# Expert weights loaded in halves, and slots narrowed to 3,264 columns

## The chip, the cores and the metric

The kernel runs on one core of one Trainium2 chip. All data is fp32. The metric is the device time of one execution in microseconds (us). A core has five engines with instruction queues of their own: PE (TensorE, matrix products), DVE (VectorE), ACT (ScalarE), POOL (GpSimd) and SP (SyncE, which here only issues DMAs). They meet through semaphores. DMAs that SP, ACT and POOL issue are carried out by the same 16 DMA engines. An indirect DMA (a scatter by row numbers) is issued by POOL.

## The reference

Two blocks in a row. The first is a linear recurrence over 768 steps for 4 batches and 8 heads of 48; the second routes each of the 3,072 resulting rows of 384 to one of 16 experts, chosen in two stages (group, then expert in the group), each expert being two matrices with a ReLU between.

```python
# recurrence: r, k, v are [4, 8, 768, 48], w and u are [8, 48]
for t in range(S):
    cur = einsum('bhd,bhe->bhde', u * kt, vt)
    y[:, :, t] = einsum('bhd,bhde->bhe', rt, state + cur)
    state = w * state + einsum('bhd,bhe->bhde', kt, vt)
x = y.transpose(0, 2, 1, 3).reshape(3072, 384)
# routing and experts: w1[g, e] is [384, 1024], w2[g, e] is [1024, 384]
for g in range(4):
    for e in range(4):            # the rows whose best group is g and best expert in it is e
        h = maximum(xg[mask_e] @ w1[g, e], 0)
        out[tok_idx] = (g_w * e_w)[:, None] * (h @ w2[g, e])
```

## The kernel before

**Recurrence.** The 768 steps are cut into 6 chunks of 128, which with 4 batches makes 24 tiles. A software pipeline runs 27 steps, `s` = 0 to 26 (loop at L852). In step `s` the kernel turns tile `s` (`turn`, L716), forms the scores of tile `s-1` (`scores`: matmul L730, masked copy L735), the values of tile `s-2` (`values`: matmuls L751, L758 and L770, copy `yT` L764 on ACT) and turns tile `s-3` back into rows (`back`, matmuls L795 and L803). Later steps also carry the routing of finished rows: logits, choice, gate, place, and then `rows` (L457), a POOL scatter of 128 rows with their gate and number into the DRAM tensor `x_sorted`, which holds one region per expert. All five engines follow a written order in this part; nothing is reordered.

**Which experts first.** After four chunks the two experts that have the most rows so far are picked (`pick_first`). Their weights are loaded while the recurrence still runs: w1 of the first at the start of step 21 (`load_w1`, L484: four DMAs of 384 KB, one for each 32 partitions, each row of 4 KB), its rows (`load_rows`, L548 and L554) and w2 (`load_w2`, L489: one DMA of 1,536 KB) at the end of step 21, w1 of the second at the start of step 24. The row load waits until the scatters of those rows have landed. SP issues these in order, so what stands behind a waiting DMA on SP waits too.

**Two places for weights.** `places[0]` is a pair of tiles of its own (`w` in the profile); `places[1]` lies over the buffers of k and r (`kall` and `rall`), which the recurrence no longer needs by then. Expert number `e` in the sorted order uses place `e % 2`. A second copy of w2 with the columns regrouped (`w_parts`) is made by ACT, and for the first expert partly by POOL (`w2_part`, L480, four copies an expert).

**Experts.** There are 17 items: the first 128 rows of the first expert (item 0, run inside the last steps of the recurrence), the rest of its rows (item 1), then one item for each of the other 15 experts. Rows of an item are columns of its matmuls: `columns` (L561) turns the rows on DVE, `up` (L596) makes two 128-blocks of the hidden layer from w1 at a call (`f` = 0, 2, 4, 6), ACT applies the ReLU (L600), and `down` (L617) makes one of three 128-blocks of the output (`d`), which ACT copies (L620). `SLOTS` says how many columns the item of the n-th expert has. Were an expert to have more rows than its slot, the rows beyond it would be done by a slow part at the end. PE and DVE follow the written order here too; the order of ACT, POOL and SP comes from the scheduler. PE's order for item `i` is

```python
up(i, 0); up(i, 2); down(i - 1, 1); up(i, 4); up(i, 6); down(i - 1, 2); down(i, 0)
```

with item 1 and the last item differing a little: item 1 has no output of an earlier item between, so `down(1, 0)` follows `up(1, 6)` at once. After `up(i, 6)` SP loads the rows of item `i + 2`, and after `down(i, 0)` it loads w1 and w2 of the expert that follows in the same place (`load_expert`). The output goes out by `pieces_out`: one POOL scatter (L656) for each 32 columns of the item, 104 in all, and for the last item by `rows_out`: two POOL scatters (L669), one of 128 rows and one of the rest.

**DMA bookkeeping.** DMAs issued by SP take their completion semaphores in turn from eight; before one is issued, SP waits until the DMA that last used its semaphore has landed.

Of the kernel before, what the change touches and what calls it, by code (L numbers as in the profile page):

```python
# [9 lines left out]
I32 = mybir.dt.int32  # L10
# [6 lines left out]

SLOTS = [256, 240, 233, 222, 216, 212, 206, 202, 199, 196, 193, 190, 187, 184, 178, 173]  # L20
CAP = max(SLOTS)
FOUR = 4

# [11 lines left out]
def kernel(  # L35
# [13 lines left out]
    nc = tc.nc  # L49
# [43 lines left out]
    def cst(shape, name, dtype=FP32):  # L93
        return const.tile(shape, dtype, name=name)
# [387 lines left out]
    def load_w1(e, i):  # L482
        for q in range(P // BL):
            nc.sync.dma_start(  # L484
                out=places[i][0][BL * q : BL * (q + 1)], in_=w1f[bass.ds(e, 1), q].rearrange("a p k f -> (a p) k f")
            )

    def load_w2(e, i):
        nc.sync.dma_start(out=places[i][1], in_=w2f[bass.ds(e, 1)].rearrange("a p k f -> (a p) k f"))  # L489

    def load_expert(e, i):

        load_w1(e, i)
        load_w2(e, i)
        return places[i]

    def transposed(x, dst):
# [18 lines left out]
    def parts(i):  # L516
        return [min(P, width(i) - a) for a in range(0, width(i), P)]
# [7 lines left out]
    def is_last(i):  # L525
        return i == len(ITEMS) - 1

    def padded(n):
        return -(-n // BL) * BL

    def load_rows(i, expert, queue, other=None):

# [30 lines left out]
    def keys_in(i):  # L563
        key = xgs.pop(i)[1]
        w = padded(width(i))
        ids = item_tile(i, [P, room(i) // BL], "ids", U32, bufs=4)
        gates = item_tile(i, [P, room(i) // BL], "gates", bufs=4)
        if is_last(i):
            for j, n in enumerate(parts(i)):
                nc.vector.tensor_scalar(  # L570
                    out=ids[0:n, j : j + 1], in0=key[0:n, j, ROW_ID : ROW_ID + 1], scalar1=float(N), scalar2=None,
                    op0=OP.add,
                )
                nc.vector.tensor_copy(gates[0:n, j : j + 1], key[0:n, j, ROW_GATE : ROW_GATE + 1])
# [49 lines left out]
    def turn_out(i, d0, d1):  # L624

        if d0 == 0:
            out_rows[i] = [
                (bank([P, DM], "pb"), item_tile(i, [P, DM], "yt", bufs=4)) for j in range(len(parts(i)))
            ]
        gates = keys_of[i][1]  # L630
# [32 lines left out]
    def rows_out(i, d0=0):  # L663
        turn_out(i, d0, KO)
        ids = keys_of[i][0]
        for j, n in enumerate(parts(i)):
            yt = out_rows[i][j][1]

            ins = nc.gpsimd.indirect_dma_start(  # L669
                out=out, out_offset=bass.IndirectOffsetOnAxis(ap=ids[0:n, j : j + 1], axis=0), in_=yt[0:n],  # L670
                in_offset=None, bounds_check=N - 1, oob_is_err=False,
            )
            tc.declare_no_dep(ins.ins, group="rows out", reason="no token comes twice")
            tc.add_to_no_dep_group("rows out", ins.ins)
# [170 lines left out]
    def expert_of(number, engines):  # L845
        return nc.values_load(
            number, engines=engines, min_val=0, max_val=GE - 1,
            skip_runtime_bounds_check_because="four bits of a whole number",
        )

    LAST = 3
    for s in range(NT + LAST):  # L852
        pieces = todo.pop(s, [])
# [39 lines left out]
        if s == FOUR * B + 5:  # L893
            first = expert_of(first_i[0:1, 0:1], (SP,))
            second = expert_of(first_i[0:1, 1:2], (SP,))
            load_w1(first, 0)
        if s == NT:
            columns(0)
            load_w1(second, 1)
        run("first")  # L900
        if s < NT:
            turn(s)
# [28 lines left out]
            values(s - 2)  # L931
        run("last")
        if s == FOUR * B + 5:
            load_rows(0, first, nc.sync)
            load_w2(first, 0)
            weights[0] = places[0]
        n = s - 3
        if n >= NT - B:
            row_logits(n)
# [48 lines left out]

    warm(13, bank([P, P], "idle"))
    load_rows(2, second, nc.sync)  # L990
    load_w2(second, 1)
    weights[1] = places[1]
    written.close()
    alive.close()
# [2 lines left out]
    with ExitStack() as moe:  # L997
        pools[1] = moe.enter_context(tc.tile_pool(name="moe", bufs=2, reuse_waits="tile"))
        w2_parts.append(pools[1].tile([P, FO, KO, P], FP32, bufs=1, name="w2_parts_1"))
        with tc.manual_schedule(engines={mybir.EngineType.PE, mybir.EngineType.DVE}):  # L1000
            columns(1)
            keys_in(0)
            pieces_out(0)
            keys_in(1)


            for i in range(1, len(ITEMS)):
                left_over = [lambda d=d: down(i - 1, d) for d in (1, 2)] if i > 1 else []

                def go_on():  # L1010
                    if left_over:
                        left_over.pop(0)()
                        if not left_over:
                            pieces_out(i - 1)

                up(i, 0)
                if is_last(i):
                    go_on()
                up(i, 2)
                go_on()  # L1020
                up(i, 4)
                up(i, 6)
                e = ITEMS[i][0] + 2
# [12 lines left out]
            rows_out(i, 2)  # L1036

# [229 lines left out]
```

## Time and profile before

| | |
|---|---|
| median of 4 runs | 433.42 us (431.75 to 434.56) |
| the profiled execution, its own time | 434.66 us |
| its span, first to last instruction | 432.9 us |
| mean granted TensorE clock in it | 0.989 |
| busy: PE, PEld, DVE, ACT, POOL | 412.7, 385.9, 183.6, 216.3, 202.4 us |
| DMA: packets, bytes, mean rate | 124,476, 86.67 MB, 200 GB/s |

Times in the trace are counted from the start of the span. PE is the matrix product, PEld the loading of its stationary operand; an fp32 product appears as two MATMUL records. The recurrence with its routing fills the span up to about 164 us, items 1 to 16 the rest. A wait put down to "remote" is one for a semaphore whose sender the profile could not place, and "issue" is time in which an engine waited for nothing that the profile shows. DMA share is the mean busy share of the 16 DMA engines; it can read a little over 1.

### The profile page before, as it was taken

How to read it: one execution, taken by the hardware profiler on the slowest of the kernel's cores; microseconds unless marked ns; L12 is line 12 of the kernel's file. 1: busy time of each engine (PE TensorE's matmuls, PEld its weight loads, DVE VectorE, ACT ScalarE, POOL GpSimd, SP SyncE). 2: the span in 40 equal slices, each digit the busy share in tenths (PEclk: the TensorE clock that was granted, in tenths of full speed). 3: DMA queues.
4: the chain of work that ended last, by engine and by line, in shares of the span. 5: the costliest groups of instructions: out<-in, count | busy, mean ns of one | idle time of the engine just before them, and what ended most of it. 6: DMA issues, size and time to landing. Idle time of an engine off the chain costs nothing. (4 is left out here: it accounts for less than half of the span.)

```text
span 432.9 us, 9930 instructions
## 1 busy us (share of the span) xinstructions
PE 412.7 (95%) x3649; PEld 385.9 (89%) x3649; DVE 183.6 (42%) x620; ACT 216.3 (50%) x505; POOL 202.4 (47%) x214
## 2 busy tenths in 40 slices
PE   7799999999989897999999999999999999999993
PEld 6688888888867697999999999999999999999993
DVE  6666879787948555030303303213213213303211
ACT  2796766777657311526335163463363464365340
POOL 6875557677670633030426245254254255335453
PEclk9999999999998999899999999999999999999998
DMA  9999999991196829997979779899899899999001
GB/s 173 212 249 267 301 246 209 217 185 40 46 231 186 201 82 238 249 221 199 247 170 278 154 217 258 191 253 225 220 257 223 224 247 250 227 262 273 21 25 35
DMA packets 124476, 86.67 MB, mean 200 GB/s; under 512 B 96998, under 2 KB 113565, under 8 KB 124420
## 3 DMA queue, kind: packets, MB, share of 16 engines
q1 hardware_dynamic: 112732, 69.05, 70.7%
q0 software_dynamic: 4960, 9.48, 6.8%
q10 hardware_dynamic: 6728, 7.44, 5.0%
q8 instruction: 30, 0.49, 0.5%
q14 instruction: 26, 0.21, 0.2%
HBM read 70.15 MB, written 16.44 MB: 200 GB/s over the span
## 5 line engine op out<-in xcount | busy, mean ns | idle before, releaser
L656 POOL DMA_INDIRECT out_dram<-yp,ids x104 | 101.2, 974 | 164.2 <-DVE yo L611 128.6
L617 PE MATMUL po<-hT,w_parts 128*128 128x128 f32 (+15 forms) x816 | 139.7, 328 | 2.0 <-ACT hT L600 2.0
L617 PEld LDWEIGHTS po<-hT,w_parts 128*128 128x128 f32 x816 | 133.8, 190 | 3.2 <-ACT hT L600 2.2
L649 DVE STREAM_TRANSPOSE yr<-yo 128x224 f32<-128x224 f32 (+3 forms) x48 | 22.0, 464 | 185.9 <-ACT yo L620 180.7
L596 PE MATMUL ph<-xe,w 128*128 128x128 f32 (+7 forms) x432 | 72.1, 322 | 1.5 <-issue 0.8
L596 PEld LDWEIGHTS ph<-xe,w 128*128 128x128 f32 x432 | 68.7, 190 | 2.8 <-issue 1.4
L596 PE MATMUL ph<-xe,kall 128*128 128x240 f32 (+7 forms) x384 | 70.2, 340 | 0.0
L600 ACT ACTIVATE hT<-ph 128x256 f32<-128x256 f32 (+15 forms) x68 | 33.5, 496 | 71.0 <-PE ph L596 50.1
L596 PEld LDWEIGHTS ph<-xe,kall 128*128 128x128 f32 x384 | 66.6, 193 | 1.0
L620 ACT COPY yo<-po 128x128 f32<-128x128 f32 (+15 forms) x51 | 16.2, 321 | 90.3 <-PE po L617 61.3
L705 ACT ACTIVATE am<-ident,du 128x128 f32<-128x128 f32 x192 | 58.7, 391 | 2.0 <-DVE du L697 1.8
L735 DVE COPY_PREDICATED am<-later,pa 128x512 f32<-128x512 uint32 x48 | 32.7, 728 | 16.1 <-PE pa L730 8.9
L480 ACT COPY w_parts<-rall 128x768 f32<-128x768 f32 x32 | 38.0, 1235 | 0.0
L457 POOL DMA_INDIRECT x_sorted<-xt,place_i x24 | 23.8, 994 | 25.4 <-DVE rb L822 14.0
L480 ACT COPY w_parts<-w 128x768 f32<-128x768 f32 x29 | 34.4, 1233 | 0.0
L691 POOL TENSOR_TENSOR dg<-rall,kall 128x768 f32<-128x768 f32 (+1 forms) x13 | 22.1, 1702 | 21.6 <-DVE du L697 21.1
L730 PE MATMUL pa<-rT,kT 48*128 48x128 f32 x384 | 30.2, 286 | 1.5 <-issue 1.4
L730 PEld LDWEIGHTS pa<-rT,kT 48*128 48x128 f32 x384 | 24.3, 187 | 4.2 <-issue 2.5
L758 PE MATMUL py<-am,vt 128*64 128x128 f32 x384 | 26.4, 279 | 0.0
L684 POOL TENSOR_TENSOR kh<-kall,T 128x768 f32<-128x768 f32 (+1 forms) x12 | 21.7, 1806 | 9.9 <-PE pu L770 3.6
L720 ACT COPY kT<-pk 128x512 f32<-128x512 f32 x24 | 14.0, 584 | 22.0 <-PE pk L716 19.7
L758 PEld LDWEIGHTS py<-am,vt 128*64 128x64 f32 x384 | 20.5, 136 | 4.2 <-issue 3.5
(146 smaller groups left out, 408.5 us busy)
## 6 DMA issues: line engine op xcount, KB each, us to landing
w<-in_moe_w_dram SPq DMA_DIRECT2D x32, 384.0 KB
w<-in_moe_w_dram SPq DMA_DIRECT2D x8, 1536.0 KB
kall<-in_moe_w_dram SPq DMA_DIRECT2D x32, 384.0 KB
rall<-in_moe_w_dram SPq DMA_DIRECT2D x8, 1536.0 KB
x_sorted<-nothing ACTq DMA_DIRECT2D x4, 1544.0 KB
rall<-in_r_dram SPq DMA_DIRECT2D x12, 384.0 KB
vt<-in_v_dram SPq DMA_DIRECT2D x12, 384.0 KB
kall<-in_k_dram SPq DMA_DIRECT2D x10, 384.0 KB
```

The source lines that it names most:

```text
L457: ins = nc.gpsimd.indirect_dma_start(out=xs_dram, out_offset=bass.IndirectOffsetOnAxis(ap=place_i[:, i : i + 1], axis=0), in_=xt[:, i, :], ...
L480: copy(w2_parts[e % 2][:, a : a + 2], w2[:, a : a + 2, :].rearrange("p f (c k) -> p f k c", k=KO))
L596: nc.tensor.matmul(ph[:, q, :], lhsT=w1[:, ko, P * (f + q) : P * (f + q + 1)], rhs=xe[:, ko, 0:w], start=(ko == 0), stop=(ko == KO - 1), s ...
L600: nc.scalar.activation(hTs[i][:, f : f + 2, 0:w], ph, AF.Relu)
L617: nc.tensor.matmul(po, lhsT=w2[:, fo, d, :], rhs=hT[:, fo, 0:w], start=(fo == 0), stop=(fo == FO - 1))
L649: nc.vector.transpose(yr[:, 0:b, :, d], y[:, d, 0:w].rearrange("p (b t) -> p b t", t=BL))
L656: ins = nc.gpsimd.indirect_dma_start(out=out_pieces, out_offset=bass.IndirectOffsetOnAxis(ap=ids[:, j : j + 1], axis=0), in_=yp[:, j], in_ ...
L691: engine.tensor_mul(dg, rts[g % RING][:, a0:a1, :, 0:D], kts[g % RING][:, a0:a1])
L705: nc.scalar.mul(am[:, e, hc, :], ident, dus[n // 2][:, n % 2, h : h + 1])
L730: nc.tensor.matmul(pa[e][:, hc, :], lhsT=kT[rows, hc, :], rhs=rT[rows, hc, :], start=True, stop=True, skip_group_check=True,)
L735: nc.vector.copy_predicated(am[:, e], earlier, pa[e])
L758: nc.tensor.matmul(py[e][DP * o : DP * (o + 1), j, :], lhsT=vt[:, a, 4 * o + 2 * j + e, :], rhs=am[:, e, 2 * o + j, :], start=(c == 0), st ...
```

## The change

Three things are changed.

1. **Loading by halves.** `load_w1` and `load_w2` take a half: the first or last 512 hidden units. w1 becomes eight DMAs of 192 KB with rows of 2 KB, w2 two DMAs of 768 KB. The number of bytes is the same.
2. **When they are issued.** In the recurrence: w1 of the first expert, half 0 at the start of step 21 and half 1 at step 22; its rows and w2 half 0 at the end of step 22 instead of 21; w2 half 1 at step 24; w1 of the second expert, half 0 at step 25 and half 1 at step 26. All but the first of these take the expert's number from a small copy that POOL makes in that step (`at_step`), so SP cannot issue them before POOL has come to that copy. Both halves of the second expert's w2 stay where the whole was. In the experts: w1 half 0 is issued after `up(i, 2)` instead of after `down(i, 0)`, w2 half 0, the rows, and the other two halves after `up(i, 6)`.
3. **Slots.** Eleven of the 16 slots get narrower, together 3,287 columns before and 3,264 after. The last item's second scatter, of 45 rows before, would have 41; it is rounded up to 48, the rows beyond the item having a row number that the scatter's bounds leave out.

The order of instructions on PE and DVE stays, apart from two small memsets on DVE for the 48 rows. On POOL four copies of one number are added: two after the fifth scatter of the run of L457 that comes first, one after the four that follow, one after the next two. On ACT the scheduler now puts two of the four `w_parts` copies of an item ahead of the ReLU of `up(i, 0)`, and the other two between those of `up(i, 4)` and `up(i, 6)`; before, they stood after the ReLUs of `up(i, 0)` and `up(i, 2)`. On SP an expert has 15 DMAs instead of 10.

```diff
-SLOTS = [256, 240, 233, 222, 216, 212, 206, 202, 199, 196, 193, 190, 187, 184, 178, 173]
+SLOTS = [256, 237, 233, 220, 214, 209, 205, 202, 199, 194, 193, 189, 185, 183, 176, 169]
...
+    FH, FOH = F // 2, FO // 2
+
+    def load_w1(e, i, half):
+        units = slice(FH * half, FH * (half + 1))
         for q in range(P // BL):
             nc.sync.dma_start(
...
+                out=places[i][0][BL * q : BL * (q + 1), :, units],
+                in_=w1f[bass.ds(e, 1), q, :, :, units].rearrange("a p k f -> (a p) k f"),
+            )
+
+    def load_w2(e, i, half):
+        blocks = slice(FOH * half, FOH * (half + 1))
+        nc.sync.dma_start(
+            out=places[i][1][:, blocks], in_=w2f[bass.ds(e, 1), :, blocks].rearrange("a p k f -> (a p) k f")
+        )
...
+    def sixteens(n):
+
+        return -(-n // 16) * 16
...
         if is_last(i):
+
+            nc.vector.memset(ids, N)
...
-            yt = out_rows[i][j][1]
+            yt, n = out_rows[i][j][1], sixteens(n)
...
+    def at_step(s, j):
+
+        number = cst([1, 1], f"number_{s}", I32)
+        nc.gpsimd.tensor_copy(number, first_i[0:1, j : j + 1])
+        return expert_of(number, (SP,))
...
-            load_w1(first, 0)
+            load_w1(first, 0, 0)
+        if s == FOUR * B + 6:
+            load_w1(at_step(s, 0), 0, 1)
         if s == NT:
             columns(0)
-            load_w1(second, 1)
+            load_w2(at_step(s, 0), 0, 1)
+        if s in (NT + 1, NT + 2):
+            load_w1(at_step(s, 1), 1, s - NT - 1)
...
         if s == FOUR * B + 5:
+            weights[0] = places[0]
+        if s == FOUR * B + 6:
             load_rows(0, first, nc.sync)
-            load_w2(first, 0)
-            weights[0] = places[0]
+            load_w2(first, 0, 0)
...
                 up(i, 2)
+                e = ITEMS[i][0] + 2
+                if e < GE:
+                    expert = expert_of(order_i[0:1, e : e + 1], (SP,))
+                    load_w1(expert, e % 2, 0)
                 go_on()
                 up(i, 4)
                 up(i, 6)
...
                 if e < GE:
-                    expert = expert_of(order_i[0:1, e : e + 1], (SP,))
+                    load_w2(expert, e % 2, 0)
                     load_rows(i + 2, expert, nc.sync)
+                    load_w1(expert, e % 2, 1)
+                    load_w2(expert, e % 2, 1)
+                    weights[e] = places[e % 2]
                 go_on()
                 down(i, 0)
...
-            if e < GE:
-                weights[e] = load_expert(expert, e % 2)
```

More of the change, by code (lines that the diff above doesn't have):

```diff
@@ L480, in w2_part @@
         copy(w2_parts[e % 2][:, a : a + 2], w2[:, a : a + 2, :].rearrange("p f (c k) -> p f k c", k=KO))
-    def load_w1(e, i):
+    FH, FOH = F // 2, FO // 2
+    def load_w1(e, i, half):
+        units = slice(FH * half, FH * (half + 1))
         for q in range(P // BL):
             nc.sync.dma_start(
-                out=places[i][0][BL * q : BL * (q + 1)], in_=w1f[bass.ds(e, 1), q].rearrange("a p k f -> (a p) k f")
-            )
-    def load_w2(e, i):
-        nc.sync.dma_start(out=places[i][1], in_=w2f[bass.ds(e, 1)].rearrange("a p k f -> (a p) k f"))
+                out=places[i][0][BL * q : BL * (q + 1), :, units],
+                in_=w1f[bass.ds(e, 1), q, :, :, units].rearrange("a p k f -> (a p) k f"),
+            )
+    def load_w2(e, i, half):
[3 more added lines that the diff above has]
+        )
     def load_expert(e, i):
-        load_w1(e, i)
-        load_w2(e, i)
+        for half in range(2):
+            load_w1(e, i, half)
+            load_w2(e, i, half)
         return places[i]
@@ L629, in turn_out @@
             ]
+            for j, n in enumerate(parts(i)):
+                if n < sixteens(n):
+                    nc.vector.memset(out_rows[i][j][1][n // BL * BL : sixteens(n)], 0.0)
         gates = keys_of[i][1]
@@ L990 @@
     load_rows(2, second, nc.sync)
-    load_w2(second, 1)
+    for half in range(2):
+        load_w2(second, 1, half)
     weights[1] = places[1]
@@ L1022 @@
                 up(i, 6)
-                e = ITEMS[i][0] + 2
                 if e < GE:
-                    expert = expert_of(order_i[0:1, e : e + 1], (SP,))
+                    load_w2(expert, e % 2, 0)
                     load_rows(i + 2, expert, nc.sync)
+                    load_w1(expert, e % 2, 1)
+                    load_w2(expert, e % 2, 1)
+                    weights[e] = places[e % 2]
                 go_on()
```

## The prediction

> **What bounds the kernel now.** I read the windows first, in stretches of 2 to 20 us.
>
> ```profile
> 120.00:122.00 2.00, 2.00 (x39) 1.82 (x36) 1.21 (x7) 1.78 (x7) 1.92 (x2) 1.00 1.02 199
> 126.00:128.00 2.00, 1.10 (x5) 0.52 (x5) 0.00 (x0) 0.47 (x2) 1.39 (x3) 1.00 0.94 309
> 130.00:132.00 2.00, 2.00 (x12) 2.00 (x11) 2.00 (x3) 0.73 (x3) 0.00 (x0) 0.50 0.01 4
> 136.00:141.00 5.00, 4.85 (x67) 3.57 (x65) 3.64 (x12) 3.76 (x15) 0.00 (x0) 1.00 1.06 351
> 145.00:147.00 2.00, 1.69 (x14) 1.30 (x11) 0.70 (x3) 0.00 (x0) 1.58 (x2) 1.00 1.06 206
> 169.00:173.00 4.00, 2.07 (x19) 1.88 (x17) 0.73 (x6) 0.32 (x1) 2.13 (x3) 1.00 1.14 315
> 173.00:178.00 5.00, 4.88 (x18) 4.30 (x19) 0.35 (x1) 0.35 (x3) 0.00 (x0) 0.66 1.01 228
> 300.00:320.00 20.00, 20.00 (x120) 20.00 (x119) 4.31 (x16) 10.72 (x16) 9.63 (x11) 1.00 0.94 248
> ```
>
> Columns are the stretch, its length, busy time of PE, PEld, DVE, ACT and POOL, then clock, DMA share, GB/s. From about 178 to 420 us PE is full at clock 1.00, as in the last line, with the DMA engines at 0.7 to 1.0 beside it: the experts are bound by PE, and a transfer there is hidden. Between 120 and 178 us PE has three holes, at 126, 146 and 171 us; the first and third are followed by half clock. Next the timelines of PE and POOL, and the waits, for these holes.
>
> ```profile
> 125.17 0.71 PE L730 MATMUL pa<-rT,kT 48*128 48x128 f32 x7
> 126.04 0.36 PE L730 MATMUL pa<-rT,kT 48*128 48x128 f32 x1 [0.16 <-issue]
> ...
> 129.60 1.09 PE L716 MATMUL pr<-ident,rall 128*128 128x128 f32 x4 [0.46 <-issue]
> ```
> ```profile
> 122.44 1.01 POOL L457 DMA_INDIRECT x_sorted<-xt,place_i  x1
> ...
> 127.58 0.98 POOL L457 DMA_INDIRECT x_sorted<-xt,place_i  x1 [0.30 <-issue]
> 142.56 0.97 POOL L457 DMA_INDIRECT x_sorted<-xt,place_i  x1 [13.99 <-DVE rb L822]
> ...
> 146.40 0.98 POOL L457 DMA_INDIRECT x_sorted<-xt,place_i  x1 [0.30 <-issue]
> ```
> ```profile
> DVE xe L561 <- DMA xg<-x_sorted: 5.8, 1, 5.8
> DVE am L735 <- PE pa L730: 5.0, 1, 5.0
> ACT yT L764 <- remote: 4.5, 1, 4.5
> ACT hT L600 <- remote: 3.9, 1, 3.9
> ```
>
> In all three holes POOL issues a run of four or five scatters while a burst of weights fills the DMA engines: scatters 122.4 to 128.6 beside w1 of the first expert (issued at 117.5), 142.6 to 147.4 beside w2 of the first and w1 of the second, 166.9 to 171.7 (L656) beside w2 of the second. In the first two PE crawls, "issue" being its reason; in all three a consumer sees a finished product 3 to 5 us late (the last three waits), until about 1 us after the run's last scatter: 129.6, 148.3, 172.7. Runs of seven scatters at 405.7 and 416.6 us, with a DMA share of 0.10 and 0.06, leave PE full. That both together are needed is my reading, not shown.
>
> The price of the first hole: step 22 begins at 121.62 and step 23 at 129.60. The work of a step here, added from its rows, is 4.7 us, so 3.3 us are lost; step 23 at half clock takes 6.6 us to 136.16 where 4.85 are work, 1.7 more. Second: the values at 144.1 are done at 145.2, ACT copies them at 148.43, and `back` starts at 148.86 where `up(0, 2)` without gaps (1.35 us after 145.6) would let it start at 147.0: 1.9 us. Third: 2.05 us of waiting, and 24 products in 6.71 us instead of 4.86: 3.9 us.
>
> **The change, part by part.**
>
> *Slots (term A).* Two forms of L617 give the price of a column:
>
> ```profile
> L617 PE MATMUL po<-hT,w_parts 128*128 128x240 f32 x48 | 10.2, 366 | 0.0
> L617 PE MATMUL po<-hT,w_parts 128*128 128x173 f32 x48 | 7.4, 310 | 0.0
> ```
>
> (366 - 310) / 67 = 0.836 ns a column and record; an item has 48 records in `up` and 48 in `down`, so 80 ns a column. 23 columns: -1.85 us, all on the path, since PE is full. It would need a row count above a slot to cost anything; the reference's routing gives 206 and 211 rows for the two first experts (slots 256 and 237) and 208 down to 162 for the others, each 1 to 25 below its slot. The 48-row scatter against 45 and two memsets (some 0.1 us each on DVE, as L611) are under 0.1 us.
>
> *Bursts in the recurrence (B, C).* w1 moved 1,536 KB at about 200 GB/s, 7.7 us; half 0 alone takes 3.9 and is over near 122.8, as the first scatter of the run starts. Half 1 waits on SP for POOL's copy after the fifth scatter, 128.6 us. So the run of scatters finds free engines, and I expect the first hole gone: -3.3 - 1.7 = -5.0. Now something else is late: the rows of item 0 stand behind half 1 on SP and in the queue: 129.3 first issue, bytes 130.7 to 134.5, then 192 KB of rows to about 136. `columns(0)` in DVE's written order ran at 137.75 and, 5 us earlier, would be wanted at 132.8. DVE waits some 3.4 us there; but behind it stand 0.5 + 1.65 + 0.24 + 1.33 us (L800, the gate to place, L822, L735) before the masked scores that the last `values` needs, so these are ready near 140.5 instead of 143.2 and PE fills the wait with `up(0, 0)` only after 136.9. Of the 5.0 I keep 3.0; ends 0 and -5.0.
>
> w2 of the first expert is now through by 140 and w1 of the second not issued until POOL has made its second run (142.6 to 147.4 before): no burst, so the second hole goes too, -1.9. A lag of near 1 us without a burst is in the trace (the product done at 422.8 us is evicted at 423.87), so I take -1.2; ends 0 and -1.9.
>
> *The last scatters (D).* The end of the recurrence is a chain: last scatter 157.56 to 158.54, row load issued at 160.67, DVE's `columns(1)` at 163.74 (the 5.8 us wait), PE at 164.10, with 26 idle products as filler. Half 1 of the second expert's w1 is now released on POOL by the copy just ahead of those two scatters and is 3.9 us of bytes in their way. The packets in the trace say that in the first hole no scatter byte moved until 125.9, when the burst ended, 3.5 us after its issue; without a burst it took 1.3 to 1.5. So the two scatters end up to 3.9 us late; since the copy comes some 2.4 us ahead of them, I take +1.5; ends 0 and +3.9.
>
> The Trainium skill ("DMA: Bandwidth & Descriptors", Queues, rings and completion order) says that each DMA engine goes round between queues packet by packet; by that the scatter would only share and term D would be near +0.5. The 125.9 above speaks against it.
>
> *The third hole (E).* Its scatters and its burst (w2 of the second, now two DMAs issued together) keep their places, so it stays: 0. But w1 half 0 of the third expert now follows at once instead of at 172.7 us, so the burst does not end with the scatters. Lags under a continuous burst in the experts are up to 3.9 us (a ReLU that started at 305.76 for a product done at 301.8); ends -0.5 and +2, I take +0.2.
>
> *The experts.* The loads there start a quarter of an item earlier, and 15 DMAs instead of 10 stand in the queue of SP; ACT's `w_parts` copies move. Each costs nothing while PE stays full. The cover: the weights of an expert are asked for more than one item (14 to 19 us) ahead. The moved pair of copies (2 x 1.23 us) puts the last ReLU some 1 us later, and `down(i-1, 2)` (2.4 to 3 us) plus six of eight blocks of `down(i, 0)` lie between. New on SP: w2 half 0 waits for ACT's first two copies, with the row load and the second halves queued behind it; the rows are wanted an item later. If this cover failed, one late item costs what it is late, and 14 of them the same each time.
>
> The same page (Rules for kernel authors) asks for at least 1 MiB a DMA and 128 partitions, and its fit of 2.0 us + bytes / 436e3 would make eight 192 KB pieces some 20 us, longer than any item and a loss of several us in each; my estimate from that page. The row at 120 us shows 384 KB pieces of 32 partitions already back to back at a share of 1.02, so pieces do not pay one by one, but at 199 GB/s against 351 for w2 at 136 us.
>
> **Sum.** -1.85 - 3.0 - 1.2 + 1.5 + 0.2 = -4.35. Made against the profiled execution's own 434.66 this is 430.3 for one like it; that execution lies 1.24 above the median of the runs, so on the median of 433.42 it is 429.1.
>
> **Rivals.** (1) *Only the columns.* The holes come from the scatters alone, or the wait of `columns(0)` and D eat what B and C give: 433.42 - 1.85 = 431.6. For it: the rows do come later on SP. Against: the full PE at 405 us. (2) *The halves block the row chain.* Half 1 of the second expert delays the last scatters by its whole 3.9 us, while the first holes shrink little (B + C at -0.5 because the rows of item 0 now gate them): 433.42 - 1.85 - 0.5 + 3.9 = 435.0. It decides from the point where the delay D passes 2.35 us. For it: the 5.8 us wait of DVE L561 is already the end of that part, and anything on it counts in full. (3) *Both holes go whole and the scatters slip through*: 433.42 - 1.85 - 5.0 - 1.9 = 424.7 at most; some 426.5 with D at its middle.
>
> **How the numbers follow.** This kernel's measurement can tell about 0.5%, 2.2 us, from no change. Chances: the forecast, 428 to 431.2, 0.46; rival 3, below 428, 0.20; rival 1, 431.2 to 433.4, 0.20; rival 2 and other losses 0.14. Faster by over 0.5% (below 431.25) 0.66, same (to 435.6) 0.24, slower 0.10. The range reaches from rival 3's middle less 0.5, 426.0, to 433.6, where the losses begin to outweigh the columns.
>
> **What would show it.** Right: no gap in PE between 122 and 136 us with clock 1.00; step 23 within 5.5 us of step 22; the ACT wait at L764 of 4.5 us gone; DVE L561 waiting 2 to 4 us on `xg` near 133 us, a wait that is not there now; PE's first product on `kall` at 169 to 171 instead of 173.67; from there to the last product 1.85 us less. Wrong: the same crawl in scatter runs with a DMA share below 0.3 (then the scatters alone make it), `columns(1)` no earlier than 163.7, or PE below 20.00 in a stretch after 190 us.

## The result: slower by 0.28%, and the profile after

The change makes the kernel slower: 434.37 us (median of 52 runs, 432.38 to 436.79) against 433.11 us (78 runs), a ratio of 1.0028 with a 95% interval of 1.0018 to 1.0038. The forecast was 429.1. The profiled execution took 435.31 us with a span of 433.6, against 434.66 and 432.9 before.

The windows after the change, columns as before (stretch, its length, busy PE, PEld, DVE, ACT, POOL, then clock, DMA share, GB/s):

```profile
122.00:124.00 2.00, 2.00 (x28) 1.59 (x25) 1.87 (x7) 0.79 (x2) 1.74 (x2) 1.00 0.20 37
126.00:128.00 2.00, 1.32 (x13) 0.80 (x11) 0.00 (x0) 0.89 (x4) 1.42 (x2) 1.00 0.39 142
128.00:130.00 2.00, 1.01 (x5) 0.55 (x5) 0.00 (x0) 0.00 (x0) 1.27 (x3) 1.00 0.48 182
147.00:149.00 2.00, 1.08 (x9) 0.66 (x7) 0.00 (x0) 0.70 (x4) 2.00 (x4) 1.00 0.32 108
152.00:160.00 8.00, 8.00 (x62) 8.00 (x61) 5.28 (x32) 1.09 (x4) 3.48 (x5) 0.83 0.83 206
320.00:340.00 20.00, 19.58 (x118) 19.20 (x118) 4.38 (x17) 8.14 (x14) 8.37 (x9) 1.00 0.94 242
360.00:380.00 20.00, 19.77 (x126) 19.50 (x125) 7.23 (x31) 9.50 (x14) 9.24 (x10) 1.00 1.01 233
```

The change did to the transfers what the prediction said: w1's half 0 is through at 122.8 us, and the DMA engines are mostly idle (0.20 to 0.48) while POOL issues its first run of scatters, 122.87 to 129.0. Yet PE has the same hole, 1.32 and 1.01 of 2 us, and the second hole at 147 us stands beside a share of 0.32. What the engines move there are the scatters' own bytes: the queue that carries weights has no packet from 122.8 to 130.6 us. The last two lines are new; before had there

```profile
320.00:340.00 20.00, 20.00 (x123) 20.00 (x122) 4.36 (x17) 9.71 (x15) 8.53 (x9) 1.00 0.96 244
360.00:380.00 20.00, 20.00 (x128) 20.00 (x127) 6.60 (x30) 9.05 (x15) 9.95 (x11) 1.00 0.99 236
```

The timelines of PE and ACT and the waits say the same of the first two holes:

```profile
127.21 0.50 PE L749 MATMUL pa<-rT,kT 48*128 48x128 f32 x4 [0.26 <-issue]
128.66 0.27 PE L749 MATMUL pa<-rT,kT 48*128 48x128 f32 x1 [0.95 <-issue]
```
```profile
130.24 0.65 ACT L783 COPY yT<-py 128x256 f32<-128x256 f32 x2 [3.35 <-PE pr L735]
```
```profile
DVE am L754 <- PE pr L735: 5.1, 1, 5.1
ACT yT L783 <- remote: 4.5, 1, 4.5
ACT hT L616 <- remote: 3.9, 1, 3.9
```

Three waits of 5.1, 4.5 and 3.9 us, where before had 5.0, 4.5 and 3.9. PE tells the other engines by a semaphore that a product is done, and the trace also records when each increment of this semaphore takes effect. A product of the values that ended at 125.22 was seen at 130.16, 4.9 us later and 1.2 us after the run's last scatter; in the second run one that ended at 144.60 was seen at 148.22, 3.6 us later and 1.0 us after the last scatter. Between, PE's increments did not get through. Some increments are missing from the record, so a late one is counted here only where the consumer started late too or where none is missing beside it.

From the first product of item 3 to the end, 20 columns fewer should have saved 1.6 us; the stretch took 241.29 us instead of 241.05, and what lies ahead of it became 0.4 us longer. A gap is counted here as what the distance between the starts of two products exceeds the usual distance of their form by. By this count PE lost 1.65 us in nine gaps of 0.03 to 0.58 us, all in `up(i, 6)` of five items between 306 and 372 us; before has none.

### The profile page after: what moved, and what is told of

Same layout as the page of the kernel before. It is cut to its first block, busy times and chain, and to the rows that moved or that the text cites. A ratio compares the mean times of both kernels' runs of the same rounds, so it can differ in the third digit from the quotient of the medians.

```text
span 433.6 us, 10228 instructions
## 1 busy us (share of the span) xinstructions
PE 413.4 (95%) x3649; PEld 385.7 (89%) x3649; DVE 184.5 (43%) x622; ACT 214.3 (49%) x505; POOL 202.7 (47%) x218
## 5 line engine op out<-in xcount | busy, mean ns | idle before, releaser
L633 PE MATMUL po<-hT,w_parts 128*128 128x128 f32 (+15 forms) x816 | 138.7, 326 | 2.1 <-ACT hT L616 2.1
L633 PEld LDWEIGHTS po<-hT,w_parts 128*128 128x128 f32 x816 | 133.0, 190 | 3.1 <-ACT hT L616 2.3
L612 PE MATMUL ph<-xe,w 128*128 128x128 f32 (+7 forms) x432 | 74.0, 327 | 1.5 <-issue 1.4
L612 PEld LDWEIGHTS ph<-xe,w 128*128 128x128 f32 x432 | 70.0, 196 | 3.2 <-issue 2.4
L612 PE MATMUL ph<-xe,kall 128*128 128x237 f32 (+7 forms) x384 | 70.0, 339 | 0.0
L457 POOL DMA_INDIRECT x_sorted<-xt,place_i x24 | 23.9, 994 | 23.7 <-DVE rb L841 13.1
```

What stands on the lines that cost most here:

```text
L457: ins = nc.gpsimd.indirect_dma_start(out=xs_dram, out_offset=bass.IndirectOffsetOnAxis(ap=place_i[:, i : i + 1], axis=0), in_=xt[:, i, :], ...
L612: nc.tensor.matmul(ph[:, q, :], lhsT=w1[:, ko, P * (f + q) : P * (f + q + 1)], rhs=xe[:, ko, 0:w], start=(ko == 0), stop=(ko == KO - 1), s ...
L633: nc.tensor.matmul(po, lhsT=w2[:, fo, d, :], rhs=hT[:, fo, 0:w], start=(fo == 0), stop=(fo == FO - 1))
```

## The experiments

Each ratio is to the kernel before on the same chip. The runs fell on six chips, and these were of two kinds, which matters more than any edit here. In the runs e1 to e4 and e13 to e18 the kernel before takes 430 to 433 us, and PE's increments come up to 5 us late in every long run of scatters, as in the first profile. In e5 to e12 it takes 422.6 to 423.0 us, and no increment is more than 0.1 us late. I call this *with* and *without the lag*. What makes the difference, no run shows; only one chip was used at two times (e1 to e4 and e17, both with the lag), so it is not even shown that it belongs to the chip.

**The parts alone, with the lag.** e1: only the slots and the 48-row scatter.

```diff
-SLOTS = [256, 240, 233, 222, 216, 212, 206, 202, 199, 196, 193, 190, 187, 184, 178, 173]
+SLOTS = [256, 237, 233, 220, 214, 209, 205, 202, 199, 194, 193, 189, 185, 183, 176, 169]
```

> The kernel before with the 16 new slots and the 48-row last scatter alone; all loads as before. By the 80 ns a column of the prediction: 23 columns, -1.85 us, ratio 0.9957, whichever theory of the holes holds, since no load and no scatter moves. The rival for the lost 1.5 us of the experts says that narrower items make PE outrun its feed by themselves: then PE has gaps over 10 ns between 300 and 380 us here too and the gain is only some 0.4 us, ratio 0.999.

Measured 431.31 against 433.2 us, ratio 0.9954 (0.9931 to 0.9977), no gaps in PE between 180 and 400 us. Term A holds, and narrow items alone do not stall PE.

e2: only the experts' loop by halves (the last part of the diff above), old slots.

> The kernel before with the loads of experts 2 to 15 by halves at their new places, old slots, recurrence as before. If the halves in the experts' loop cost the gaps seen in PE after the change (1.46 us between 300 and 380 us, and 0.2 in the tail), the time rises by 1.2 to 1.7 us, ratio 1.003 to 1.004, and gaps over 10 ns stand in the last up pair of an item. If the cause is the narrower items, or the recurrence, ratio 1.000. The prediction's price for this part was 0.

Measured 434.69 us, ratio 1.0043 (1.0018 to 1.0067), with 1.33 us of gaps. One of them, from PE's timeline of this run, and its windows:

```profile
336.80 1.47 PE L620 MATMUL ph<-xe,w 128*128 128x193 f32 x8
338.58 1.47 PE L620 MATMUL ph<-xe,w 128*128 128x193 f32 x8 [0.30 <-issue]
```
```profile
320.00:340.00 20.00, 19.70 (x120) 19.47 (x119) 4.77 (x17) 8.97 (x15) 7.79 (x8) 1.00 0.87 213
360.00:380.00 20.00, 19.75 (x125) 19.61 (x124) 6.53 (x30) 10.13 (x15) 9.73 (x10) 1.00 0.98 240
```

PE stops in the middle of a chain of products, with no wait that the profile names. The part that I had priced at nothing costs about as much as the slots bring. (The scheduler moved ACT's copies here as in the kernel after; e14 takes that apart.)

e3: only the recurrence's loads by halves.

> The kernel before with the two first experts' weights by halves, one a step, old slots, whole loads in the experts' loop. Prediction (a hole needs scatters and a burst): -2.7 us, ratio 0.994, step 23 within 5.5 us of step 22. Scatters alone: both holes stay, and what is left is the later last scatter, +0.3 to +0.8 us, ratio 1.001 to 1.002.

Measured 433.93 us, ratio 1.0012 (0.9989 to 1.0035); all three holes stay, with waits of 5.0, 4.5 and 3.9 us. The forecast 0.994 is out; what "scatters alone" expected is what came, though the interval includes no change. Its DMA share beside the first run is 0.45 and 0.36 (126 to 130 us), as in the kernel after.

e4: weights whole, the two loads of w1 at their old times, but the runs of scatters to be broken up; the row load of item 0 and w2 of the first expert are issued two steps later, behind the scatters. `between` holds the last two scatters of the second run.

```diff
-                when.append((when[5][0] + (1 + i if n < FOUR * B - 1 else 0), "last"))
+                late = 1 + i if n < FOUR * B - 1 else (i + 1) // 2 if n == FOUR * B - 1 else 0
+                when.append((when[5][0] + late, "last"))
...
             for a in (0, 2, 4):
                 w2_part(0, a, nc.gpsimd.tensor_copy)
+                if between:
+                    between.pop(0)()
```

> The kernel before with its weight loads in whole pieces and at their old times, but with POOL's two long runs of scatters broken: the four scatters of the group that picks the first expert go out as 1, 2 and 1 in steps 21, 22 and 23 (the row load of item 0 and w2 follow in step 23), and two of the four of the next group stand between the three copies of w2 that POOL makes in step 25. Scatters alone: no run is longer than 3, the lag of PE's semaphore goes from 5 us to about 1 (as after the pairs at 90, 101 and 112 us), the first hole and its half clock go (-3 to -5 us) and the second shrinks (-1 to -1.9): 427 to 429.5, ratio 0.985 to 0.992. Scatters plus burst: w1 is under way beside every scatter as before, so the crawl stays where scatters and w1 meet (122 to 126 us) and the gain is under 1 us, ratio 0.998 or above. Rival: the later row load of item 0 makes DVE wait at its columns and gives the gain back.

Measured 430.94 us, ratio 0.9943 (0.9921 to 0.9964). The edit for the first run failed: POOL has nothing else to do in steps 22 and 23, so it still issued five scatters back to back (122.26 to 128.4) and the first hole stayed. The gain is the second run's: with copies of 1.25 us between its scatters the increments got through 0.7 us after the first pair and the second hole closed, while w1 of the second expert moved beside it at full rate as before (share 1.05 from 145 to 147 us). Part of the gain is hidden: in the tail of its profiled run a product that ended at 416.41 was seen at 418.77, 2.4 us later (1.0 for the same product in before), and the last scatter comes 1.3 us later behind item 16's start.

**The same questions without the lag.** e5: the first run really broken, by a one-element copy on POOL that reads the step's `yT`, with `columns(0)` later.

```diff
+        if s == NT:
+            columns(0)
+        if s in (FOUR * B + 6, FOUR * B + 7):
+            nc.gpsimd.tensor_copy(cst([1, 1], f"mark_{s}"), yTs[s - 2][0:1, 0, 0, 0:1])
         run("last")
```

> The kernel before (whole loads, old slots) with the first run of scatters really broken up: in steps 22 and 23 a one-element copy on POOL reads that step's yT ahead of the step's scatters, so POOL can't run ahead; two scatters go in step 21, two in 22, one in 23. The row load of item 0 and w2 follow in step 23, and columns(0) stands behind the values of step 24. Scatters alone: PE's increments are held only for the 2.3 us of a pair and 0.7 after it, the crawl at 126 to 129.6 us goes and step 23 begins within 6 us of step 22: -1.5 to -3.5 us, ratio 0.992 to 0.997, less whatever DVE waits for item 0's rows. Scatters plus burst: w1 is still under way beside the first pair, the gain is under 0.5 us, ratio 0.999 to 1.001.

Measured 429.89 against 422.56 us, ratio 1.0169 (1.0150 to 1.0189). On this chip there was no hole to take away, and the rival named there is all that is left: the rows of item 0 come later, DVE waits 4.79 us for them before 141.27, and the recurrence's chain with it. The window of this run:

```profile
136.00:141.00 5.00, 2.55 (x33) 1.97 (x29) 0.48 (x2) 1.60 (x6) 0.00 (x0) 1.00 0.19 44
```

e6: the output scatters of item 0 behind the first product of item 2.

```diff
             keys_in(0)
-            pieces_out(0)
             keys_in(1)
...
                 up(i, 0)
+                if i == 2:
+                    pieces_out(0)
```

> The kernel before with one move: pieces_out(0), the output scatters of item 0 (166.9 to 171.7 us), comes after the first product of item 2. Scatters alone: the third hole goes, PE's 2.05 us of waiting between 169 and 173 us and in part the half clock behind it; the same run of four then falls where PE has several items of work in hand: -1.5 to -3.5 us, ratio 0.992 to 0.9965. If the hole came from the burst of w2 (whole, same time): it stays, ratio 1.000.

Measured 422.59 us, ratio 0.9998 (0.9989 to 1.0007); e10 repeated it on another chip, also without the lag.

> The run with pieces_out(0) behind the first product of item 2 again. Where PE's increments lag: the third hole goes, -1.5 to -3.5 us, ratio 0.992 to 0.9965; if the burst of w2 makes the hole, ratio 1.000. Where they don't lag there is no third hole to take away: ratio 1.000, as measured before, and the run tells nothing new.

Measured ratio 1.0002 (0.9993 to 1.0011). What e10 is worth lies in its trace, which up to 160 us is the kernel before on such a chip. POOL's first run and PE's window beside it:

```profile
123.62 0.97 POOL L457 DMA_INDIRECT x_sorted<-xt,place_i  x1 [0.31 <-issue]
124.89 0.97 POOL L457 DMA_INDIRECT x_sorted<-xt,place_i  x1 [0.30 <-issue]
126.17 0.97 POOL L457 DMA_INDIRECT x_sorted<-xt,place_i  x1 [0.31 <-issue]
```
```profile
124.00:126.00 2.00, 2.00 (x26) 1.88 (x25) 0.98 (x2) 1.46 (x6) 1.56 (x2) 1.00 1.01 292
126.00:128.00 2.00, 2.00 (x41) 1.46 (x41) 1.97 (x5) 1.55 (x5) 0.97 (x1) 1.00 0.57 205
```

The same five scatters, the same burst of weights (share 1.01), and PE is full. So even both together make no hole by themselves; a hole needs the late increments, which appear only in some of the runs. The three holes that I priced before at 3.3 + 1.7, 1.9 and 3.9 us add up to 10.8; the kernel before is 10.6 us faster here (433.2 - 422.6).

e7 and e8 cross the loads in the experts' loop with ACT's order, which the scheduler had changed along with them. e7 has halves with ACT's old order, e8 whole loads with the new one (both with ACT written out by hand in the loop). The two added lines are e7's, where the copies stand behind the ReLU, and e8's, where they stand ahead of it.

```diff
-            for a in {2: (0,), 4: (2,), 6: (4, 6)}.get(f, ()):
+            for a in {0: (0, 2), 2: (4, 6)}.get(f, ()):
+            for a in {0: (0, 2), 6: (4, 6)}.get(f, ()):
```

> The kernel of the loop run (halves in the experts' loop, old slots) with ACT's order in the loop written out as the kernel before has it: two copies of w2 behind the ReLU of units 0, two behind that of units 2. If the gaps in PE come from ACT's moved copies: ratio 1.000 and no gaps over 40 ns between 300 and 400 us. If they come from the loads by halves (smaller packets, other times, SP's waits): the loss stays at +1.2 to +1.9 us, ratio 1.003 to 1.004, and the gaps with it.

> The other corner: the kernel before with whole loads at their old times, and ACT's order in the loop written out as the kernel after has it: two copies of w2 ahead of the ReLU of units 0, two between those of units 4 and 6. If ACT's order makes the gaps: +1.2 to +1.9 us, ratio 1.003 to 1.004, gaps between 300 and 400 us. If the loads make them: ratio 1.000 and no gaps.

Measured 0.9994 (0.9985 to 1.0003) and 0.9998 (0.9989 to 1.0007), no gaps between 300 and 400 us in either. Without the lag neither can tell anything of the gaps.

e9: the kernel after itself, without the lag.

> The kernel after, unchanged, to see whether its loss hangs on the late increments of PE's semaphore. In the runs of the first job (before at 433.2 us) PE's increments came up to 5 us late in every run of scatters; in those of the second (before at 422.6) no lag passed 0.5 us and no hole stood at 126, 146 or 171 us. If the lag is what the change's halves lose to: where the lag is present, ratio 1.002 to 1.004 as recorded; where it is absent (before near 422.6), only the columns count, less the chain of the last scatters, -1.85 + 0 to 0.6, ratio 0.9956 to 0.997. If the loss comes from the loads themselves, it is 1.002 to 1.004 in both.

Measured 427.98 against 422.96 us, ratio 1.0112 (1.0094 to 1.0130): slower by 5 us, which none of the three expectations had. PE has no gaps in the experts, so these need the lag; the loss is in the recurrence's end. The windows of this run, then SP and POOL in its timeline, then SP in that of e10:

```profile
152.00:160.00 8.00, 4.53 (x41) 4.34 (x39) 0.00 (x0) 0.60 (x3) 0.46 (x1) 1.00 0.67 173
160.00:169.00 9.00, 8.34 (x48) 8.34 (x49) 5.86 (x34) 1.15 (x3) 3.88 (x4) 0.62 0.68 199
```
```profile
150.53 1.84 SPq L489 DMA_DIRECT2D kall<-in_moe_w_dram  x4
157.38 0.83 SPq L562 DMA_DIRECT2D xg<-x_sorted  x2
```
```profile
151.49 0.97 POOL L457 DMA_INDIRECT x_sorted<-xt,place_i  x1 [0.30 <-issue]
```
```profile
153.49 0.83 SPq L571 DMA_DIRECT2D xg<-x_sorted  x2
```

The last scatter is issued at 151.49, half 1 of the second expert's w1 at 150.53 to 152.4 beside it. By the packets the last scatter moved no byte before 154.5, and the row load that waits for it came at 157.38; in e10, without half 1 there, it came 3.05 us after the scatter (150.44 to 153.49) and not 5.9. PE idles 3.5 us in the first window and then runs at a clock of 0.62. The 3.9 us of the row load and up to 3.4 for 6.83 us at half clock, less 1.85 for the columns, make up to 5.5 of loss; 5.0 were measured.

e11 is e7 on this chip: ratio 1.0002 (0.9991 to 1.0013), nothing new.

> Halves in the experts' loop with ACT's order written out as the kernel before has it, again. Where PE's increments lag: if the gaps in PE (1.2 us in the loop run) come from ACT's moved copies, ratio 1.000 and no gaps; if from the loads by halves, 1.003 to 1.004 and the gaps stay. Where they don't lag: 1.000 either way, as measured before.

e12: a version to beat both, slots of e1, the broken second run of e4 and the later scatters of e6, whole loads.

> A version meant to beat both: the kernel before with whole loads, plus the new slots and the 48-row scatter (-1.9 us measured), two of the four scatters at 142 us moved between POOL's three copies of w2 (-2.3 us measured with them there), and pieces_out(0) behind the first product of item 2. Where PE's increments lag: -1.9 - 2.3 - 1.5 to -3.5, less overlap: -4 to -7 us, ratio 0.984 to 0.991. Where they don't lag: only the columns, -1.85, ratio 0.9956; the two moves are worth 0 there.

Measured 421.65 us, ratio 0.9974 (0.9962 to 0.9986): faster than before, by 1.1 us (from the ratio) of the 1.85 that the columns alone should give. What takes the rest, no run shows.

**With the lag again.** e13: the kernel after with half 1 of the second expert's w1 behind the rows of item 1.

```diff
-        if s in (NT + 1, NT + 2):
-            load_w1(at_step(s, 1), 1, s - NT - 1)
+        if s == NT + 1:
+            load_w1(at_step(s, 1), 1, 0)
...
+    load_w1(second, 1, 1)
     load_rows(2, second, nc.sync)
```

> The kernel after with one change: half 1 of the second expert's w1 is issued at the end of the recurrence, behind the rows of item 1, and no longer beside the last two scatters. In the run of the kernel after without the lag (e9_after) the last scatter was issued at 151.5 us as before, half 1 at 150.5 to 152.1, and the row load that waits for the scatters came at 157.4 instead of 153.5. If that is the whole loss: the row load is back at 153.5 to 154, the 3.9 us and the half clock behind them go, and only the columns (-1.85) and small waits remain: ratio 0.996 to 0.999 without the lag; with it the loss of 0.56 at the last scatter goes and the experts' gaps stay, 0.999 to 1.002. If the wait of DVE for item 0's rows (133 to 136 us) is a second cause, it stays at 1.002 to 1.005 without the lag.

Measured 433.36 against 433.29 us, ratio 0.9992 (0.9971 to 1.0013). The row load follows the last scatter by 3.06 us, as before (3.11; 3.31 in the kernel after, 3.79 in e3), and 1.19 us of gaps in the experts stay. The loss of e9 was not tried with this edit without the lag.

e14 is e7 with the lag.

> Halves in the experts' loop with ACT's order written out as the kernel before has it, a third time. With the lag: if the gaps in PE (1.2 us in the loop run) come from ACT's moved copies, ratio 1.000 and no gaps between 300 and 400 us; if from the loads by halves, 1.003 to 1.004 and the gaps stay. Without the lag 1.000, as measured twice.

Measured 435.6 us, ratio 1.0051 (1.0026 to 1.0077), with 1.31 us of gaps. ACT's moved copies are not their cause. A second loss lies in the tail: the last scatter comes 24.0 us after the first product of item 16, 22.6 in before. The hand-written order of ACT is not shown to cause it, though the output scatters of item 15 begin later under it (12.8 us after that product, 10.5 in before): e4 and e16, where the scheduler orders ACT, have the last scatter at 23.9 and 24.0 too. As in e4 a late increment lies there: a product that ended at 425.73 was seen at 427.55 (at once in before).

e15 is e12 with the lag.

> Columns, the two scatters between POOL's copies of w2, and the output scatters of item 0 later, again. Without the lag it was 0.9974 (0.9962 to 0.9986) and should be so again. With the lag: -1.9 for the columns, -2.3 for the two scatters, -1.5 to -3.5 for the third hole, less overlap: ratio 0.984 to 0.991; if only columns and the two scatters count, 0.990.

Measured 425.81 against 433.29 us, ratio 0.9834 (0.9804 to 0.9865), 7.5 us faster. Its windows:

```profile
126.00:128.00 2.00, 1.09 (x7) 0.55 (x6) 0.00 (x0) 0.36 (x2) 1.49 (x2) 1.00 0.88 306
145.00:147.00 2.00, 2.00 (x24) 1.68 (x24) 1.13 (x8) 1.17 (x5) 1.83 (x3) 1.00 1.05 203
169.00:173.00 4.00, 4.00 (x24) 3.82 (x23) 0.00 (x0) 2.08 (x3) 2.00 (x3) 1.00 1.13 211
```

The first hole, which it leaves alone, is there; the second and third are gone, beside DMA shares of 1.05 and 1.13.

**Size or time of the halves.** e16: loads of the experts by halves, at the old place and in the old order of bytes.

```diff
-                    load_w1_whole(expert, e % 2)
-                    load_w2_whole(expert, e % 2)
+                    for half in range(2):
+                        load_w1(expert, e % 2, half)
+                    for half in range(2):
+                        load_w2(expert, e % 2, half)
```

> The kernel before with the weights of experts 2 to 15 still loaded by halves, but all at the old place behind the item's first down product, in the old order of bytes (both halves of w1, then both of w2). Where PE's increments lag: if size or number of the DMAs makes the gaps, ratio 1.003 to 1.005 and over 1 us of gaps between 300 and 400 us; if their time makes them, ratio 1.000 and none. Where they don't lag, 1.000 either way.

Measured 449.86 against 433.33 us, ratio 1.0398 (1.0363 to 1.0432). The question got no answer: the scheduler now put ACT's copies of w2 behind the ReLUs of units 4 and 6, `down` waited for them, and with the lag on top items of 206 to 187 columns all took 17.5 to 17.8 us instead of 16.9 to 15.3.

e17: the same with ACT's old order written out.

> The kernel before with all loads of experts 2 to 15 by halves at the old place and in the old order of bytes, and ACT's order written out as before has it: only the size and number of the DMAs differ from before. If ACT's late copies made the 16.5 us of the last run, they are gone here. Where PE's increments lag: if size or number of the DMAs makes the gaps of the change, ratio 1.003 to 1.005 and about 1.2 us of gaps between 300 and 400 us; if only their time does, ratio 1.000 and none. Where they don't lag: 1.000 either way.

Measured 431.72 against 430.13 us, ratio 1.0040 (1.0025 to 1.0056), but with one gap of 0.09 us in all. Its windows:

```profile
320.00:340.00 20.00, 20.00 (x123) 20.00 (x123) 5.00 (x18) 8.35 (x14) 6.82 (x7) 1.00 0.87 226
360.00:380.00 20.00, 20.00 (x128) 20.00 (x127) 3.86 (x16) 10.28 (x15) 10.12 (x11) 1.00 0.93 240
```

So 2 KB rows and 15 DMAs at the old place do not make the gaps. Most of the ratio is the tail, as in e14: the last scatter is 1.3 us later from item 16's start than in before. The other corner, whole loads at the new times, was not run.

e18: e14 with the runs of output scatters broken; POOL's order is written out too.

```diff
             tc.add_to_no_dep_group("rows out", ins.ins)
+            if i > 0 and j % 2 and j < b - 1:
+                nc.gpsimd.tensor_copy(spacer[:, 0:640], spacer[:, 640:1280])
```

> The kernel of e14 (halves in the experts' loop, ACT's order as in before, old slots) with a POOL copy of 640 elements a partition between every second and third output scatter of an item, so that no run of them is longer than two. Where PE's increments lag: if the runs of scatters are what makes the gaps, the lags fall to about 1 us, the 1.2 us of gaps between 300 and 400 us go, and the ratio falls from 1.0051 to 1.000 or 1.001; if the gaps come from the loads alone, 1.004 to 1.005. Where they don't lag: 1.000. Rival: the copies lengthen POOL's work in an item by some 3 us, to about 12 us, and if that makes the scatters late for the tiles they read, the time rises.

Measured 434.58 against 430.13 us, ratio 1.0114 (1.0085 to 1.0142). The gaps are gone, no increment in the experts is more than 0.8 us late, and items 3 to 15 keep the pace of the kernel before to 0.01 us:

```profile
320.00:340.00 20.00, 20.00 (x123) 20.00 (x122) 4.29 (x16) 7.92 (x13) 9.72 (x11) 1.00 1.02 246
```

So gaps of over a microsecond came only with three things together: the lag, long runs of scatters, and halves at the new times. Smaller ones also come otherwise: e4, with whole loads at the old times, has 0.15 us of them at 215 us. The time lost elsewhere is only partly placed: the profiled run, the fastest of six, ends 5.6 us after its last scatter where before ends 3.4 after, 2.4 us of it a wait of SP for PE's queue; the rest of the 4.5 us stays open.

## Why the prediction was wrong, by its steps

**Term A was right.** By form, `L633` at 237 and 169 columns:

```profile
L633 PE MATMUL po<-hT,w_parts 128*128 128x237 f32 x45 | 9.5, 363 | 0.0
L633 PE MATMUL po<-hT,w_parts 128*128 128x169 f32 x48 | 7.2, 307 | 0.0
```

(363 - 307) / 68 = 0.824 ns a column and record against 0.836, and e1 alone gives 1.9 us against 1.85.

**Term B failed at "the run of scatters finds free engines, and I expect the first hole gone".** The engines were free and the hole stayed: -3.0 became 0, and DVE's `columns(0)`, which stands behind it, ran at 138.26 instead of 137.75. Term C (-1.2) failed with it. The reading "that both together are needed" rested on the full PE at 405 and 416 us. But there PE has items of work in hand, so late increments do not show in its busy time; after the change increments in the experts came up to 5.2 us late (a product that ended at 268.41 was taken up by ACT at 273.59) with PE still full. The evidence against the reading was in the trace of before: from 100.73 to 103.01 us POOL issues a pair of scatters in a stretch where hardly anything but the scatters' own bytes moves (DMA share 0.12 from 100 to 114 us), and a product that ended at 103.13 took effect at 103.72. The lag is there without any burst. It ends 0.7 to 1.2 us after the last scatter of a run of two, four or five, so a longer run holds more products back. I looked at who was busy and not at how late the products were seen.

The Trainium skill ("Perfetto Trace Analysis", Tensor Engine Instruction) says that the profiler's end of a matmul is an estimate and that the semaphore update is pushed after it and must then propagate; it gives no time for that. These runs do: at most 0.1 us without the lag, up to 5.2 us with it.

**Term D had the right mechanism and a size that depends on the lag.** Forecast +1.5 with an upper end of +3.9. With the lag the row load came 3.31 us behind the last scatter in the kernel after and 3.79 in e3, against 3.11 in before and 2.8 to 3.1 in e1, e2 and e13, so +0.2 to +1.0. The last pair of scatters also came later behind the pair ahead, 5.43 us against 4.75, but that is not half 1's doing: a stretch of half clock from 151.26 us lies there,

```profile
151.17 3.87 PE L612 MATMUL ph<-xe,w 128*128 128x128 f32 x18
```

2.17 us in before, and DVE waited for a product behind these. In e3, with the same loads and no half clock there, the distance is 4.74. Without the lag PE reaches that point earlier, the last scatter falls beside half 1, and the row load came 3.9 us later than in e10, 2.8 of it behind the scatter: the upper end. Rival 2 is that case, but its 435.0 has no term for the half clock that followed. That the 434.37 measured with the lag comes close to this figure is luck: the loss there is the experts'. As for the rule that the prediction cites from the Trainium skill ("DMA: Bandwidth & Descriptors", Queues, rings and completion order), e9 does not settle it: the last scatter's first 3 us without a byte speak against sharing, but from 154.5 to 156.5 us the packets of its queue and of the weights' queue stand side by side.

**Term E** was about right: the wait of 3.9 us stayed as it was, and the third expert's half did not lengthen it. The wait of `columns(0)` that I charged to B did not come with the lag, since B's gain did not come; without it, in e9, it is 2.71 us against my 3.4, of which e10 has 1.63 without the change.

**The experts at 0 was the second failing step**: "each costs nothing while PE stays full". What the forecast put at 0 cost 1.3 us of gaps in e2, 1.65 in the kernel after, and e2's ratio says 1.9. I had looked for data that would come late, and PE stalled with its data there. The ends of the gaps hint at how: PE goes on 0.1 to 0.2 us before a held increment is recorded (339.38 and 339.53). The increments are also later: over 3 us in eight items of the kernel after, in two of before (up to 3.9 us), though e2 has its gaps with two as well. How the moved loads turn late increments into a stop of PE is not settled. ACT's order (e14), the size of the DMAs at the old place (e17) and the loads without the lag (e9) are excluded as causes by themselves. The 20 us that the prediction worked out for eight pieces of 192 KB did not show: with such pieces the items of e17 keep the pace of before to 0.1 us.

**Rival 1** had the right mechanism for the runs with the lag, holes from the scatters and not from the burst, and the wrong sum, since it took the experts for free as well. The parts multiply to 0.9954 x 1.0043 x 1.0012 = 1.0009, inside which the measured 1.0028 lies with its neighbours' intervals of 0.002 each.

## What to carry to other kernels

Where an engine crawls and the profile names no wait, compare the ends of its products with the times at which consumers see them, in a calm stretch too; busy shares hide a late semaphore wherever there is work in hand. Where increments come late, breaking a run of scatters with work that its engine has to do anyway helped (e15, 7.5 us together with two other edits), and moving the transfers away did not; copies added for that alone closed the gaps in the experts, but that run was slower still (e18). Keep loads out of the way of the last scatter that something waits for. When a load is moved, look at what the scheduler then does with the other engines: one moved block of copies cost 16 us here.

## What the runs showed of the hardware

- In some runs, on four of the six chips, PE's semaphore increments are held back beside a run of POOL's scatters (4.9 us for five in a row, 3.6 for four, up to 5.2 in the experts for seven, 0.6 for a pair); in the others, on two chips, they are not, and the same kernel is 10.6 us apart between them.
- A POOL copy of 0.74 us (e18) or 1.25 us (e4, e15) between pairs or single scatters is enough to let increments through.
- Ahead of the tail half clock comes in stretches of 3.41 us or twice that (6.83 in e9), and not behind each hole: the profiled run of before has two ahead of the tail (129.47 and 173.84 us), after three more than 100 us into the span (130.78, 151.26, 175.16), e1 one. The skill ("TensorE: Matmul & The Clock Gate", What's actually happening) has a free-running window of about 3.4 us; the trace agrees on the length (3.41 us). One such stretch is worth up to 1.7 us (half of 3.41), so two profiles of the same kernel can differ by more than this change does.
